# The fifth product of the second group of units 1 to 6 in the inner form, with exponentials, divisions, turns and the load of v in other slots

## The chip, the cores and the metric

The kernel runs on one core of one Trainium2 chip. The metric is the device time of one execution in microseconds; the time before is the median of three runs. The profile is one further execution under the hardware profiler. The engines are named as there: PE (matrix products), PEld (PE's loads of weights, which run beside its products), DVE (vector), ACT (scalar, with tables for functions), POOL (GpSimd) and SP (which issues DMAs).

## The reference

All data are float32. For each of 8 batches with 8 heads, 576 queries and head size 64, keys and values are pooled by 8 (72 keys), and attention is taken over them. The result, 4608 tokens by 512, goes through a layer with a periodic activation:

```python
k_p = k.reshape(B, H, Sp, pool, D).mean(axis=3)
v_p = v.reshape(B, H, Sp, pool, D).mean(axis=3)
scores = scale * np.matmul(q, k_p.transpose(0, 1, 3, 2))
scores = scores - np.max(scores, axis=-1, keepdims=True)
attn = np.exp(scores)
attn = attn / (np.sum(attn, axis=-1, keepdims=True) + 1e-09)
x = np.matmul(attn, v_p)                      # then (4608, 512)
h = x @ w_in                                  # (512, 2048)
s = np.sin(alpha * h)
g = h + s * s / (alpha + 1e-09)
out = g @ w_out                               # (2048, 512)
```

## The kernel before

**Two levels of seven products.** The products with `w_in` and `w_out` are cut into 2 x 2 blocks and done with seven block products and sums of blocks instead of eight block products (Winograd's form of Strassen's method). For `w_in` the outer blocks are two halves of the 512 inputs, two halves of the 2048 features, and two halves of 256 tokens of a unit. The nine units (u = 0 to 8) have 512 tokens each. In a unit the features go in four groups (J = 0 to 3), each of 2 x 128 features in each half. One of the seven products of one group is four matmuls of 128 x 128 weights by 256 tokens (`product`, line 866, `part` picks from the four). Its result stays in one of the banks b1, b6, b5 and b7 of the accumulation memory, which ACT copies one into the other (line 839: b6 from b1, b7 from b6, and p5 from b5) so that later products add to them. DVE then forms the blocks of h (line 838).

Some products are done in a second, inner level of the same form (`inner_product`, line 1046): seven matmuls of 128 x 128 by 128 tokens instead of four by 256 (line 1058). They come in four steps. Step a makes two products into a spare bank, and ACT copies them to the target bank (line 1062) and to a small tile m (line 1064). Step b makes two products, and ACT copies one quarter of the bank to another (line 1068). Step d makes one, and DVE adds m (line 1073). Step e makes the last two. Before the change the units 1 to 6 (`busy`) do the fifth product of the groups 2 and 3 and the first product of group 3 so (`I5, I1 = (2, 3), (3,)`). The sums of weight blocks that this needs are made once in unit 0 by POOL (`inner_w_in`, line 823 through `sums`), those of the tokens in each unit (`inner_x`).

**Slots.** `hidden(u, extra)` writes out by hand a unit's 28 slots, seven (k = 0 to 6) for each group, with one product in most. Each engine does its instructions in the order in which they are written. In group G's slots the group before, Q, is finished too: `sin` and `square` on ACT (lines 1028 and 1035, in place in the tile s), `finish` on DVE (line 1080), and `store_g`, which writes g to DRAM (line 1094). The product 1 stands in k = 0, 5 in k = 1, 6 in k = 2, 2 in k = 3, 7 in k = 4, 3 in k = 5 and 4 in k = 6. When the next group's fifth product is in the inner form, the second half of the fourth product is left to the next group's first slots.

**Attention between the slots.** `carry(u)` hangs the attention of the batch u + 1 into a unit's slots as extras: `two_scores` (slots 3 and 5) puts the scores into banks, and `shifts` on DVE subtracts the maximum into `ex` (lines 341 and 342). `exp` is four instructions on ACT in place (line 367), three of 576 columns and one of 864. `norm` sums and inverts on DVE (lines 373 and 374) and scales on POOL (line 375). `turn` transposes 32 x 32 blocks on DVE (lines 504 to 514), `move` sends the pieces to their partitions by DMA (line 524), and `all_values` multiplies with the pooled values. `load_v` asks for v (two DMAs at line 141, four at line 146), and POOL sums it by eight (`pool_rows`, line 132) in the place in its queue at which `load_v` is called.

**Tables.** Sine and exponential need different tables in ACT; a load is an instruction of its own (ACT_TABLE_LOAD), put ahead of the first instruction that needs another table than the one loaded. Squares and copies run with either.

**DMA queues.** All these DMAs are issued by SP in the order written. They use eight semaphores in turn, so that each issue also waits for the landing of the eighth before it.

Of the kernel before, what the change touches and what calls it, by code (L numbers as in the profile page):

```python
# [13 lines left out]
F32 = mybir.dt.float32  # L14
AX = mybir.AxisListType.X
AF = mybir.ActivationFunctionType
# [3 lines left out]
P = 128  # L20
# [20 lines left out]
class Kernel:  # L41
# [793 lines left out]
    def hidden(self, u, extra):  # L835
# [3 lines left out]
        copy = lambda o, x: nc.scalar.copy(out=o, in_=x)  # L839
        sin, square, early = self.sin, self.square, lambda G: G.J == (0 if G.u else 1)  # L840
        busy = 0 < u < self.B - 1
        I5, I1 = ((2, 3), (3,)) if busy else {7: ((2, 3), (2, 3)), 8: ((2, 3), (2, 3))}.get(u, ((), ()))
        split = lambda J: u == 0 and J == 2
        end = lambda J: u == 0 and J == 3

        def begin(J):
# [30 lines left out]
        for slot in range(7 * self.NJ):  # L877
# [9 lines left out]
            if k == 0:  # L887
# [3 lines left out]
                self.next = None  # L891
                if G.i5 and not N:
                    G.i5.a()
                if Q and not G.i5 and not end(J):
                    self.last_sines(Q, 2)
                extras()
                if G.i1:
                    G.i5.b()
                    self.last_sines(Q, 0)
                else:  # L900
                    product(G, 1, G.b1, True)
                    if G.i5:
                        product(Q, 4, Q.b7, part=(2, 3))
            elif k == 1:
                if not G.i1:
                    copy(G.b6[:], G.b1[:])
                if G.i5 and not G.i1:
                    self.last_sines(Q, 0)
                elif Q and not G.i1:
                    if end(J):  # L910
                        self.last_sines(Q, 2)
                    for i in (0,) if split(J) else (1, 0) if u == 0 else (0, 1):
                        squares(Q, i)
# [3 lines left out]
            elif k == 2:  # L917
                if Q and not G.i5 and not split(J):
                    self.finish(Q)
                if not G.i1:  # L920
                    extras()
                if G.i1:
                    product(G, 6, G.b6, part=(0, 1))
                    G.i5.d()
                    self.last_sines(Q, 1)
                    square(Q, 1, 0)
                    self.late = Q
                    extras()
                    self.finish_before()
                    product(G, 6, G.b6, part=(2, 3))  # L930
                elif G.i5:
                    product(G, 6, G.b6, part=(0, 1))
                    G.i5.b()
                    self.last_sines(Q, 1)
                    squares(Q, 0)
                    product(G, 6, G.b6, part=(2, 3))
                else:
                    product(G, 6, G.b6)
            elif k == 3:
                late = J == 0 and busy  # L940
                if Q and not late and not G.i5 and not split(J):
                    self.store_g(Q)
                G.p5 = self.tp.tile([P, JW, TH], F32, name="p5")
                if G.i1:
                    if not busy:
                        copy(G.b7[:], G.b6[:])
                    square(Q, 1, 1)
                    squares(Q, 0)
                    extras()
                    product(G, 2, G.b1)  # L950
                    G.i5.e()
                    copy(G.p5[:], G.b5[:])
                else:
                    copy(G.b7[:], G.b6[:])
                    if G.i5:
                        squares(Q, 1)
                        G.i5.d()
                        self.finish(Q)
                        self.store_g(Q)
                    else:  # L960
                        copy(G.p5[:], G.b5[:])
                    if split(J):
                        squares(Q, 1)
                        self.finish(Q, (0,))
                    extras()
                    product(G, 2, G.b1)
            elif k == 4:
                if G.i1 and busy:
                    copy(G.b7[:], G.b6[:])
                    self.behind_order = lambda: sin(G, 0, 0, G.b1)  # L970
                else:
                    sin(G, 0, 0, G.b1)
                if not G.i5:
                    square(G, 0, 0)
                extras()
                if G.i1:
                    self.finish(Q, (1,))
                    self.store_g(Q)
                product(G, 7, G.b7, part=(0, 1))
                if G.i5:  # L980
                    if not G.i1:
                        G.i5.e()
                        copy(G.p5[:], G.b5[:])
                    square(G, 0, 0)
                product(G, 7, G.b7, part=(2, 3))
            elif k == 5:
                add(G.g[:, 1, :, 1], G.b7[:], G.p5[:])
                extras()
                if split(J):
                    self.finish(Q, (1,))  # L990
                    self.store_g(Q)
                N = None
                if J + 1 in I1:
                    N = self.next = begin(J + 1)
                    N.i1.a()
                product(G, 3, G.b6, part=(0, 1))
                if N:
                    N.i1.b()
                product(G, 3, G.b6, part=(2, 3))
            else:  # L1000
                if J == 0 and busy and Q:
                    self.store_g(Q)
                add(G.g[:, 0, :, 1], G.b6[:], G.p5[:])
                sin(G, 1, 1, G.g[:, 1, :, 1])
                N = self.next
                last = lambda: add(G.g[:, 0, :, 0], G.b1[:], G.s[:, 0, :, 0])
                if not N:
                    last()
                    extras()
                    product(G, 4, G.b7, part=(0, 1))  # L1010
                    if J + 1 not in I5 or J + 1 in I1:
                        product(G, 4, G.b7, part=(2, 3))
                else:
                    product(G, 4, G.b7, part=(0,))
                    N.i1.d()
                    last()
                    N.i5.a()
                    product(G, 4, G.b7, part=(1, 2))
                    N.i1.e()
                    copy(N.b6[:], N.b1[:])  # L1020
                    extras()
                    product(G, 4, G.b7, part=(3,))
# [7 lines left out]
    def square(self, G, i, js):  # L1030

        for jj in range(JW):
            f = i * self.K2 // 2 + G.J * JW + jj
            x = G.s[:, i, jj, js, :]
            self.nc.scalar.activation(out=x, in_=x, func=AF.Square, scale=self.c[:, f:f + 1])  # L1035

    def last_sines(self, G, part):

# [163 lines left out]
    def carry(self, u):  # L1202
# [6 lines left out]
        if u == 0:  # L1209
# [37 lines left out]
            at(19, A.move, (3,), nc.scalar)  # L1247
            at(26, A.all_values)
            at(9, self.load_q, 2)
            at(23, lambda: self.inner_w_in(((5, 2, 4), (1, 3, 4)), (lambda w: [w[:, i * 2 * P:i * 2 * P + 2 * P] for i in range(8)])(self.q_tile(0))))  # L1250
            for e in range(2):
                at(12, self.load_k, 2, e)
                at(17, lambda e=e: self.pool_k[e]())
# [5 lines left out]
        if 0 < u < last:  # L1259
# [2 lines left out]
                at((3, 5)[i], A.two_scores, i)  # L1262
            at(6, A.two_shifts)
            for i in range(4):
                at((8, 9, 10, 10)[i], A.exp, i)
                at((9, 10, 11, 12)[i], A.norm, i)
                at((12, 13, 13, 13)[i], A.turn, i)
            at(14, A.move, range(4))
            at(6, self.load_v, b)
            at(12, lambda: self.pool_v())  # L1270
            for i in range(2):
                if b < last:
# [440 lines left out]
```

## Time and profile before

| | us |
|---|---|
| median of three runs | 900.68 |
| lowest, highest | 899.46, 901.40 |
| span of the profiled execution, first to last instruction | 896.2 |
| time of the profiled execution beside its span | not listed |
| PE busy | 890.8 |
| weight loads busy | 813.9 |
| DVE busy | 682.9 |
| ACT busy | 438.6 |
| POOL busy | 249.2 |

The units 1 to 6 take the stretch from about 82 to 409 us of the span, some 55 us each; from 513 us on PE works on the products with `w_out` alone. The granted PE clock is 1.000 over the span. In a timeline the columns are the start, the length, the engine, the line, the operation, what it writes and reads, the form, how many instructions follow each other (x), and in brackets the engine's idle time before them and what ended it. Each matmul of the program is two rows in the trace. SPq is SP's issue of a DMA, not the transfer.

### The profile page before, as it was taken

How to read it: one execution, taken by the hardware profiler on the slowest of the kernel's cores; microseconds unless marked ns; L12 is line 12 of the kernel's file. 1: busy time of each engine (PE TensorE's matmuls, PEld its weight loads, DVE VectorE, ACT ScalarE, POOL GpSimd, SP SyncE). 2: the span in 40 equal slices, each digit the busy share in tenths (PEclk: the TensorE clock that was granted, in tenths of full speed). 3: DMA queues.
4: the chain of work that ended last, by engine and by line, in shares of the span. 5: the costliest groups of instructions: out<-in, count | busy, mean ns of one | idle time of the engine just before them, and what ended most of it. 6: DMA issues, size and time to landing. Idle time of an engine off the chain costs nothing.

```text
span 896.2 us, 16276 instructions
## 1 busy us (share of the span) xinstructions
PE 890.8 (99%) x6274; PEld 813.9 (91%) x6274; DVE 682.9 (76%) x918; ACT 438.6 (49%) x1033; POOL 249.2 (28%) x265
## 2 busy tenths in 40 slices
PE   9999999999999999999999999999999999999998
PEld 6787888888888888888888999999999999999998
DVE  7786857768577675765677889898897896996885
ACT  6687776877768777687776711111111211111111
POOL 6798443825338252434523000000000000000000
PEclk9999999999999999999999999999999999999999
DMA  9857957759586585648126243716435355164002
GB/s 269 244 158 206 244 147 212 187 164 254 139 214 186 183 225 147 175 140 302 53 106 219 102 181 103 232 37 218 117 105 160 89 159 159 37 192 142 20 18 53
DMA packets 119533, 141.03 MB, mean 157 GB/s; under 512 B 45776, under 2 KB 86496, under 8 KB 119456
## 3 DMA queue, kind: packets, MB, share of 16 engines
q1 hardware_dynamic: 116288, 137.39, 52.6%
q10 hardware_dynamic: 3168, 2.61, 1.0%
q8 instruction: 50, 0.82, 0.4%
q14 instruction: 27, 0.22, 0.1%
HBM read 75.37 MB, written 47.19 MB: 137 GB/s over the span
## 4 chain that ended last, share of the span: by engine, by line
PE 99%; DVE 0%; POOL 0%; ACT 0%; issue 0%; DVEq 0%
PE PS L866 44%; PE PS L1383 43%; PE PS L1058 5%; PE PS L318 2%; PE PS L613 2%; PE PS L626 1%; PE PS L1126 0%; PE PS L571 0%; PE PS L290 0%; PE PS L425 0%; PE PS L279 0%; PE PS L479 0%; PE PS L569 0%; POOL tr L451 0%; PE PS L403 0%; PE PS L487 0%
## 5 line engine op out<-in xcount | busy, mean ns | idle before, releaser
L866 PE MATMUL PS<-home,a 128*128 128x256 f32 x1072 | 253.0, 381 | 0.1
L866 PEld LDWEIGHTS PS<-home,a 128*128 128x128 f32 x1072 | 198.4, 190 | 30.9 <-issue 4.6
L866 PE MATMUL PS<-home,as 128*128 128x256 f32 x736 | 177.2, 382 | 0.0
L866 PEld LDWEIGHTS PS<-home,as 128*128 128x128 f32 x736 | 134.5, 190 | 18.1 <-ACT PS L839 1.2
L1383 PE MATMUL PS<-s,wb 128*128 128x192 f32 x672 | 116.2, 326 | 0.0
L1035 ACT ACTIVATE s<-s,c 128x256 f32<-128x256 f32 (+1 forms) x236 | 115.5, 556 | 0.0
L1383 PEld LDWEIGHTS PS<-s,wb 128*128 128x128 f32 x672 | 110.4, 190 | 0.1
L132 POOL TENSOR_TENSOR kvin<-kvin 96x768 f32<-96x768 f32 (+3 forms) x42 | 73.4, 1747 | 69.9 <-DMA kvin<-in_v_dram 67.8
L838 DVE TENSOR_TENSOR h<-PS,p 128x512 f32<-128x512 f32 x72 | 49.2, 684 | 55.5 <-PE PS L866 35.2
L1554 ACT COPY PS<-PS 128x192 f32<-128x192 f32 x42 | 12.7, 303 | 146.2 <-PE PS L1383 130.0
L1028 ACT ACTIVATE s<-h,al 128x256 f32<-128x256 f32 x144 | 65.5, 509 | 32.6 <-DVE h L838 32.6
L1383 PE MATMUL PS<-r,wb 128*128 128x192 f32 x432 | 79.0, 326 | 0.0
L1383 PEld LDWEIGHTS PS<-r,wb 128*128 128x128 f32 x432 | 71.6, 190 | 0.0
L1383 PE MATMUL PS<-s,a 128*128 128x192 f32 x384 | 70.2, 326 | 0.0
L1028 ACT ACTIVATE s<-PS,al 128x256 f32<-128x256 f32 x144 | 60.0, 469 | 17.2 <-PE PS L866 16.5
L1383 PEld LDWEIGHTS PS<-s,a 128*128 128x128 f32 x384 | 63.7, 190 | 0.0
L1080 DVE TENSOR_TENSOR h<-PS,s 128x512 f32<-128x512 f32 x36 | 24.8, 689 | 48.6 <-ACT s L1035 48.6
L839 ACT COPY PS<-PS 128x512 f32<-128x512 f32 x72 | 41.5, 577 | 34.5 <-PE PS L866 26.7
L1080 DVE TENSOR_TENSOR h<-h,s 128x1024 f32<-128x1024 f32 x36 | 55.3, 1537 | 3.3 <-ACT s L1035 3.1
L1584 ACT COPY PS<-PS 128x192 f32<-128x192 f32 x42 | 12.7, 303 | 89.5 <-PE PS L1383 89.5
L1322 DVE TENSOR_TENSOR s<-r 128x768 f32<-128x768 f32 x54 | 51.4, 951 | 4.8 <-PE PS L1383 2.8
L1383 PE MATMUL PS<-s,we 128*128 128x192 f32 x288 | 52.7, 326 | 0.0
(244 smaller groups left out, 1401.4 us busy)
## 6 DMA issues: line engine op xcount, KB each, us to landing
g_bridge<-h SPq DMA_DIRECT2D x72, 512.0 KB
r<-g_bridge SPq DMA_DIRECT2D x15, 1536.0 KB
x<-g_bridge SPq DMA_DIRECT2D x8, 1536.0 KB
out_dram<-o SPq DMA_DIRECT2D x90, 96.0 KB
kvin<-in_k_dram SPq DMA_DIRECT2D x14, 576.0 KB
q<-in_q_dram SPq DMA_DIRECT2D x7, 1024.0 KB
kvin<-in_v_dram SPq DMA_DIRECT2D x14, 512.0 KB
aM<-tr SPq DMA_DIRECT2D x54, 92.0 KB
```

Of the source, the lines that this page charges most:

```text
L132: self.nc.gpsimd.tensor_tensor(out=t[..., 0:w] if w > D else out, in0=t[..., 0:w], in1=t[..., w:2 * w], op=OP.add)
L318: nc.tensor.matmul(ps[e][r0 + r:r0 + r + q.shape[-1], h, :], q[s], kb[s, hp, :], start=True, stop=True)
L613: nc.tensor.matmul(o[r:r + 64], w, x, start=start and i < 2, stop=False, skip_group_check=True)
L838: add = lambda o, x, y: nc.vector.tensor_tensor(out=o, in0=x, in1=y, op=OP.add)
L839: copy = lambda o, x: nc.scalar.copy(out=o, in_=x)
L866: nc.tensor.matmul(ps[:, jj, :], self.A[p][:, kk, f * P:(f + 1) * P], x[:, kk, :], start=(start and n == 0), stop=(kk == 1), skip_group_ch ...
L1028: self.nc.scalar.activation(out=G.s[:, i, jj, j, :], in_=src[:, jj], func=AF.Sin, scale=self.al[:, f:f + 1])
L1035: self.nc.scalar.activation(out=x, in_=x, func=AF.Square, scale=self.c[:, f:f + 1])
L1058: nc.tensor.matmul(o, W[m][:, G.J - J0], X[m], start=start and n == 0, stop=True, skip_group_check=True)
L1080: add = lambda o, x, y: self.nc.vector.tensor_tensor(out=o, in0=x, in1=y, op=OP.add)
L1322: tt = lambda o, x, y, op: nc.vector.tensor_tensor(out=o, in0=x, in1=y, op=op)
L1383: nc.tensor.matmul(out, W[:, J // 2, J % 2, :], A[:, J, :], start=(start and J == 0), stop=(J == self.NJ - 1), skip_group_check=True)
```

## The change

In the units 1 to 6 the group J = 1 joins those whose fifth product is in the inner form (`fast(G)` is true for it). Its slots are written out anew:

- k = 0: step a, then the sines of Q's first half (those on g), then product 1. The four matmuls of its fifth product are gone.
- k = 1: the copy into b6, a square of Q, step b, the second half of Q's fourth product (left over from J = 0), Q's sines from b7 and the wide squares.
- k = 2: half of product 6, step d, `finish(Q)`, the other half.
- k = 3: `store_g(Q)`, the copy into b7, half of product 2, step e, the extras, the copy to p5, the other half.
- k = 6: the sines of g's second half are left to J = 2, which does them in its k = 1.

The exponentials go in two runs: two in slot 6 (J = 0, k = 6) and two in slot 10, where all four were in the slots 8 to 10. Behind the first run stands a sine of one column (`sine_table`), which brings the sine's table back there. The divisions (`norm`) stand in the slots 7, 7, 10 and 12 (before 9, 10, 11 and 12), the turns in 9, 13, 13 and 13 (before 12, 13, 13 and 13). `load_v` moves from slot 6 to slot 4, ahead of a `store_g`. The sums of weights for the fifth product are made for three groups instead of two, in the same memory.

```diff
-        I5, I1 = ((2, 3), (3,)) if busy else {7: ((2, 3), (2, 3)), 8: ((2, 3), (2, 3))}.get(u, ((), ()))
+        I5, I1 = ((1, 2, 3), (3,)) if busy else {7: ((2, 3), (2, 3)), 8: ((2, 3), (2, 3))}.get(u, ((), ()))
         split = lambda J: u == 0 and J == 2
+        fast = lambda G: busy and G.J == 1
...
                 if G.i5 and not N:
                     G.i5.a()
+                if fast(G):
+                    sin(Q, 0, 1, Q.g[:, 0, :, 1])
...
                     product(G, 1, G.b1, True)
-                    if G.i5:
+                    if G.i5 and not fast(G):
                         product(Q, 4, Q.b7, part=(2, 3))
             elif k == 1:
                 if not G.i1:
                     copy(G.b6[:], G.b1[:])
-                if G.i5 and not G.i1:
+                if fast(G):
+                    square(Q, 0, 1)
+                    G.i5.b()
+                    product(Q, 4, Q.b7, part=(2, 3))
+                    self.last_sines(Q, 1)
+                    squares(Q, 1)
+                elif G.i5 and not G.i1:
+                    if fast(Q):
+                        sin(Q, 1, 1, Q.g[:, 1, :, 1])
                     self.last_sines(Q, 0)
...
+                if fast(G):
+                    product(G, 6, G.b6, part=(0, 1))
+                    G.i5.d()
+                    self.finish(Q)
                 if not G.i1:
                     extras()
-                if G.i1:
+                if fast(G):
+                    product(G, 6, G.b6, part=(2, 3))
+                elif G.i1:
...
-                if Q and not late and not G.i5 and not split(J):
+                if Q and not late and (not G.i5 or fast(G)) and not split(J):
                     self.store_g(Q)
...
-                    if G.i5:
+                    if fast(G):
+                        product(G, 2, G.b1, part=(0, 1))
+                        G.i5.e()
+                    elif G.i5:
...
                     extras()
-                    product(G, 2, G.b1)
+                    if fast(G):
+                        copy(G.p5[:], G.b5[:])
+                    product(G, 2, G.b1, part=(2, 3) if fast(G) else range(4))
...
-                if not G.i5:
+                if not G.i5 or fast(G):
                     square(G, 0, 0)
...
-                if G.i5:
+                if G.i5 and not fast(G):
...
-                sin(G, 1, 1, G.g[:, 1, :, 1])
+                if not fast(G):
+                    sin(G, 1, 1, G.g[:, 1, :, 1])
...
+    def sine_table(self):
+        self.nc.scalar.activation(out=self.sm.tile([P, 1], F32, name="order")[:], in_=self.al[:, 0:1], func=AF.Sin)
...
-            at(23, lambda: self.inner_w_in(((5, 2, 4), (1, 3, 4)), (lambda w: [w[:, i * 2 * P:i * 2 * P + 2 * P] for i in range(8)])(self.q_tile(0))))
+            at(23, lambda: self.inner_w_in(((5, 1, 4), (1, 3, 4)), (lambda w: [w[:, i * 3 * P:i * 3 * P + 3 * P] for i in range(4)] + [w[:, 12 * P + i * P:13 * P + i * P] for i in range(4)])(self.q_tile(0))))
...
             for i in range(4):
-                at((8, 9, 10, 10)[i], A.exp, i)
-                at((9, 10, 11, 12)[i], A.norm, i)
-                at((12, 13, 13, 13)[i], A.turn, i)
+                at((6,6,10,10)[i], A.exp, i)
+                at((7,7,10,12)[i], A.norm, i)
+            for i in range(4):
+                at((9,13,13,13)[i], A.turn, i)
+            at(6, self.sine_table)
             at(14, A.move, range(4))
-            at(6, self.load_v, b)
+            at(4, self.load_v, b)
```

## The prediction

> **What bounds the kernel now.** I read the page first: its busy shares and the chain that ended last. Then one unit in the window view, then the timelines of the engines for the second group (J = 1) of unit 3.
>
> ```profile
> span 896.2 us, 16276 instructions
> ...
> PE 890.8 (99%) x6274; PEld 813.9 (91%) x6274; DVE 682.9 (76%) x918; ACT 438.6 (49%) x1033; POOL 249.2 (28%) x265
> ...
> PE 99%; DVE 0%; POOL 0%; ACT 0%; issue 0%; DVEq 0%
> ```
> ```profile
> 150.59:205.66 55.07, 55.07 (x447) 47.22 (x446) 38.23 (x64) 41.13 (x96) 25.58 (x25) 1.00 0.71 192
> ```
>
> The chain is PE from end to end, and in the 55.07 us that separate a place in one unit from the same place in the next, PE is never idle; ACT is busy for 41.13. So a change is worth what it takes from PE's own work, minus what it makes PE wait. An average of 41 in 55 does not say whether ACT is free at one given place, so I follow it there.
>
> ```profile
> 207.42 3.62 PE L866 MATMUL PS<-home,a 128*128 128x256 f32 x16
> 210.87 3.62 PE L866 MATMUL PS<-home,as 128*128 128x256 f32 x16
> 214.32 3.66 PE L866 MATMUL PS<-home,a 128*128 128x256 f32 x16
> ...
> 220.41 0.39 PE L1058 MATMUL PS<-home,as 128*128 128x128 f32 x2
> 220.63 0.39 PE L1058 MATMUL PS<-last,q 128*128 128x128 f32 x2
> 220.86 2.75 PE L866 MATMUL PS<-home,a 128*128 128x256 f32 x12
> ...
> 223.45 1.09 PE L866 MATMUL PS<-home,as 128*128 128x256 f32 x4
> 224.38 0.38 PE L1058 MATMUL PS<-last,q 128*128 128x128 f32 x2
> ```
>
> Columns: start, length, what, count. Each matmul of the program is two rows of the trace. Sixteen of 256 columns start 3.45 us apart (207.42 to 210.87), 0.216 each, so a product (eight rows) takes 1.73. A product of the inner form (two rows of 128 columns) takes 0.22 (220.41 to 220.63 to 220.86: 0.45 for two). 207.42 is the fourth product of J = 0, 209.14 the first of J = 1, 210.87 its fifth and sixth, 214.32 its second and seventh, 220.41 step a of J = 2.
>
> **What PE saves.** The fifth product's 1.73 becomes seven inner products, 7 x 0.2225 = 1.56: 0.17 a unit. The row at 214.32 is 3.66 long where its like is 3.62: 0.04 is lost there to the copy into b7, which has more cover after. Together 0.21 a unit, 1.3 us over six units.
>
> **What ACT does for it.** These are its rows around the change, in the same unit and the next group:
>
> ```profile
> 205.02 0.91 ACT L1028 ACTIVATE s<-h,al 128x256 f32<-128x256 f32 x2 [0.88 <-DVE h L838]
> 208.34 0.91 ACT L1028 ACTIVATE s<-h,al 128x256 f32<-128x256 f32 x2 [2.42 <-DVE h L838]
> 209.16 0.89 ACT L1035 ACTIVATE s<-s,c 128x256 f32<-128x256 f32 x2
> 209.96 0.81 ACT L1028 ACTIVATE s<-PS,al 128x256 f32<-128x256 f32 x2
> 211.07 0.57 ACT L839 COPY PS<-PS 128x512 f32<-128x512 f32 x1 [0.30 <-PE PS L866]
> 211.55 1.33 ACT L1035 ACTIVATE s<-s,c 128x512 f32<-128x512 f32 x2
> 212.90 1.28 ACT L367 ACT_TABLE_LOAD   x1
> 214.20 1.26 ACT L367 ACTIVATE ex<-ex 128x576 f32<-128x576 f32 x2
> 215.36 0.58 ACT L839 COPY PS<-PS 128x512 f32<-128x512 f32 x1
> ...
> 221.48 0.37 ACT L1062 COPY PS<-PS 128x256 f32<-128x256 f32 x1
> 221.78 0.27 ACT L1064 COPY m<-PS 128x128 f32<-128x128 f32 x1
> 222.79 0.57 ACT L839 COPY PS<-PS 128x512 f32<-128x512 f32 x1 [0.74 <-PE PS L866]
> ...
> 225.08 0.25 ACT L1068 COPY PS<-PS 128x128 f32<-128x128 f32 x1 [0.90 <-PE PS L1058]
> ```
> ```profile
> L1121 ACT ACTIVATE one<-ident x1: 202/202/202, 3.0 to 3.0; 128x1 f32<-128x1 f32 x1
> ```
>
> Before, ACT rested from 205.93 to 208.34. After, this gap holds the first two exponentials and the sine of one column, and both need a table load, 1.28 each. Starts follow each other sooner than lengths say: a pair of sines on h holds the queue 0.82 (208.34 to 209.16), a pair of squares 0.80, a 512-wide copy 0.48, L1062's copy 0.30; the next instruction starts some 0.09 before the last ends. A load is the exception: it starts when the last has ended (211.55 + 1.33 = 212.88, load at 212.90) and holds what follows until it is done (214.20).
>
> The walk on ACT, from the sine at 205.02, whose start PE sets and which stays where it is: ends 205.93; load 205.94; two exponentials 207.24 to 208.50; load 208.51; the one-column sine 209.81, 0.20 long by the row of L1121, so the next at 209.92; step a's copy (L1062) 209.92 to 210.29; its second copy at 210.22, 0.27 long, less 0.09; the sines of the group before at 210.40; the copy from b1 to b6 at 211.21, ended 211.78; two squares at 211.69; step b's copy (L1068) 212.49, ended 212.74.
>
> The walk on PE, if nothing held it: half the fourth product from 207.42, step a 208.28, first product 208.73, step b 210.46, the other half of the fourth product 210.90, half the sixth 211.76, step d 212.63. Step b needs step a's copy (210.29), the sixth product the copy into b6 (211.78), step d step b's copy (212.74). PE asks before the matmul starts, with its weights:
>
> ```profile
> 215.99 1.59 PEld L866 LDWEIGHTS PS<-home,a 128*128 128x128 f32 x8 [0.18 <-ACT PS L839]
> ...
> 220.20 0.41 PEld L1058 LDWEIGHTS PS<-home,as 128*128 128x128 f32 x2
> ```
>
> Weights go out 0.21 ahead of the matmul (220.20, 220.41), and 0.05 after the copy that held them (215.36 + 0.58 = 215.94, 215.99). For step d: 212.74 + 0.05 + 0.21 = 213.00, and up to 0.05 more where the wait stands in an instruction of its own. Against 212.63 that is 0.37 to 0.42; I take 0.40. The smaller waits at step b (some 0.1) and at the sixth product lie inside it, for ACT runs without a gap from 205.02 to step b's copy and its end is what counts. Such holds exist already: in J = 2 the copy at 222.79 ends 223.36, the four rows at 223.45 last 1.09 and the next start 0.93 later instead of 0.87, 0.06 lost.
>
> Bounds of this price: the one-column sine could hold the queue for 0.05 only, and its neighbour 0.16 instead of 0.18: delay 0.29. Without the overlaps (0.09 twice) and with sines a tenth slower, 0.65. I take 0.40 since every other term is a row of this kind and place.
>
> **Behind step d** everything keeps its cover. ACT: the sines from b7 at 212.65, the wide squares 213.38 to 214.71, the copy into b7 at 214.62 to 215.20 (seventh product not before 216.3), load, the other two exponentials 216.50 to 217.99, the copy to p5 to 218.48, load, the sines of b1 at 219.78, squares, and step a of J = 2 at 221.3, where it was 221.48. The second pair of loads thus falls into time that had no work on PE's path; on PE's path they would cost 2.6 a unit. The sines moved from J = 1 to J = 2 (0.82) fit between the copy into b6 there and step b's copy at 225.08, which waits for PE.
>
> **DVE, POOL and SP.** DVE gains step d's add and does divisions and turns elsewhere:
>
> ```profile
> 209.91 1.06 DVE L342 TENSOR_TENSOR ex<-PS,mx 128x864 f32<-128x864 f32 x1
> 213.53 1.22 DVE L1080 TENSOR_TENSOR h<-h,s 128x1024 f32<-128x1024 f32 x1
> 217.06 0.76 DVE L373 TENSOR_REDUCE sm<-ex 128x8 f32<-128x584 f32 x1 [0.29 <-ACT ex L367]
> 218.03 0.69 DVE L838 TENSOR_TENSOR h<-PS,p 128x512 f32<-128x512 f32 x1
> 218.63 0.70 DVE L504 STREAM_TRANSPOSE tr<-ex 128x512 f32<-128x512 f32 x1
> ...
> 229.26 1.93 DVE L1080 TENSOR_TENSOR h<-h,s 128x1024 f32<-128x1024 f32 x1
> ```
> ```profile
> 211.30 4.58 POOL L132 TENSOR_TENSOR kvin<-kvin 128x1024 f32<-128x1024 f32 x2 [10.57 <-DMA kvin<-in_v_dram]
> 215.95 0.73 POOL L132 TENSOR_TENSOR vm<-kvin 128x256 f32<-128x256 f32 x1
> 216.64 3.37 POOL L375 TENSOR_TENSOR ex<-ex,sm 128x576 f32<-128x576 f32 x3
> ```
> ```profile
> 196.73 5.42 SPq L1094 DMA_DIRECT2D g_bridge<-h  x4
> 202.24 1.44 SPq L141 DMA_DIRECT2D kvin<-in_v_dram  x2
> ```
>
> DVE: shifts done 210.97, two divisions' halves (0.9 each) to 212.8, the add of step d at 213.4, the finishing adds at 214.75 (after the squares) to 216.6, the first turn (0.8) to 217.4, the third division to 218.3, then the add on b7 and p5 at 218.5 to 219.2. The second half of PE's fourth product follows at 219.36 + 0.40, so 0.4 is spare. It needs the first turn not to wait: POOL must have pooled v (5.3 from its start) and scaled the first tile (1.12) by 216.6, so v must be in SBUF by 210.1, and by 210.7 to cost nothing. It was there at 211.30. SP now asks for v ahead of two of the four stores in the row at 196.73, from about 198 instead of 202.24, and two transfers fewer lie ahead of it; I take 206 to 208. The two stores passed go out some 2 us later, and the h buffer they free is next written at 218.5. The query's load behind them waits for the scores anyway. The finishing add can last 1.93 when POOL works beside it (229.26): 0.7, inside the 0.28 before the p5 copy and the 0.4.
>
> [...]
>
> Unit 0's sums for three groups instead of two lengthen four POOL instructions by half, below 2 us once:
>
> ```profile
> 84.74 0.46 POOL L823 TENSOR_TENSOR last<-home 128x128 f32<-128x128 f32 x1 [3.66 <-DVE home L833]
> ```
>
> POOL idles 3.66 behind them, so they cost nothing.
>
> **Sum.** A unit: 0.40 - 0.21 = +0.19; six units +1.1 us, a span of 897.3 after 896.2. The median of the three runs, 900.68 (899.46 to 901.40), is 4.5 above the profiled span, which stands for the launch's rest; the profiled execution has no other time listed. Forecast 901.8, slower by 0.13%, which a measurement of this kernel can hardly tell from no change (0.2%, 1.8 us). With the bounds of the delay the likeliest case's own range is 901.2 to 903.3.
>
> **Rivals.**
> (1) ACT is in time and only the saving shows: -1.3, 899.4. It needs step b's copy ended by 212.37, 0.37 sooner. For it: the exponentials stand where ACT rested 2.4 us. Against: two loads and two exponentials take 3.9. 0.14, a third of it (waits of before that vanish besides) below 898.9.
> (2) The first turn holds DVE: v lands no sooner than 211.30, POOL's first scaling ends 217.8, turn 218.6, third division 219.5, add 220.2 instead of 219.2; PE's fourth product loses 0.6 a unit more, 3.6: 905.4. It decides from a landing after 210.7. For it: DMA is 71% busy in the unit and v takes 9 us from its issue to 211.30. Against: it is asked 4 us sooner. 0.17, with the slow finishing add.
> (3) A switch of the table holds ACT as long again as its load: 1.28 more each, 2.56 in ACT's walk, step d 2.96 late, 2.75 net a unit, 16.5 us: 917. Against: the rows at 211.55, 212.90 and 214.20 leave 0.02 on either side of the load. 0.02. [...]
> (4) The inner form runs no faster here and ACT holds nothing: 900.7. 0.05.
>
> The forecast has 0.62; some 0.22 of that, delays above 0.51, is over 902.5. Faster by over 0.2%: 0.05 of (1) and 0.02 of (4), 0.07. Slower by over 0.2%: 0.22 + 0.17 + 0.02 = 0.41. Within: 0.52. The range reaches from the saving alone, 899.4, to near (2), 904.8.
>
> **What would show it.** In the profile after: a weight load of step d in J = 1 idle before it for about 0.3 with ACT L1068's copy as its releaser, six times; four table loads a unit instead of two; ACT without a gap between the sines at the end of J = 0 and step b's copy; POOL's pooling of v starting before 210 on this unit's scale; DVE's add on b7 and p5 ready before PE's fourth product. Wrong if PE shows no idle there, or if the largest wait is DVE behind POOL.

## The result: slower, and the time after

| | us |
|---|---|
| after, median of six runs | 905.43 (902.60 to 909.03) |
| before, on the same chip, six runs | 899.11 (898.29 to 901.40) |
| ratio | 1.0066, 95% interval 1.0044 to 1.0088 |
| profiled execution after | 907.65, span 905.9 |

The kernel is slower by 0.66%, where 0.13% was forecast, and 905.43 lies above the range. Its runs also spread over 6.4 us, twice as far as those before. In the kernel after, the lines of the code have moved: L866 is now L867 (product), L1058 is L1084 (inner product), L1062, L1064 and L1068 are L1088, L1090 and L1094 (the copies of steps a and b), L1028 and L1035 are L1051 and L1058 (sine and square), L1080 is L1106, L1061 is the one-column sine.

From the page of the kernel after: the span, the busy times and the chain that ended last.

```profile
span 905.9 us, 16407 instructions
...
PE 895.1 (99%) x6310; PEld 816.3 (90%) x6310; DVE 679.3 (75%) x924; ACT 459.1 (51%) x1069; POOL 245.1 (27%) x265
...
PE 98%; issue 1%; DMA 0%; DVE 0%; POOL 0%; ACTq 0%; ACT 0%; DVEq 0%; POOLq 0%
```

The chain is PE still, with one new part: 1% "issue", in which PE waited for nothing that the profile shows. It is not spread evenly. In the window view, cut where PE begins the value products (L613) of each unit, the columns are the stretch, its length, the busy time of each engine, the granted clock, the DMA share and GB/s:

```profile
132.52:187.71 55.19, 55.19 (x455) 47.09 (x458) 37.86 (x65) 44.47 (x102) 24.77 (x25) 1.00 0.67 192
187.71:246.66 58.95, 56.89 (x456) 48.40 (x458) 37.54 (x65) 44.73 (x102) 24.76 (x25) 0.97 0.64 180
246.66:302.05 55.39, 55.39 (x455) 47.02 (x458) 37.92 (x65) 44.47 (x102) 24.77 (x25) 1.00 0.66 191
302.05:359.67 57.62, 55.12 (x455) 47.47 (x458) 37.66 (x65) 44.62 (x102) 24.73 (x25) 1.00 0.65 184
359.67:414.87 55.20, 55.20 (x455) 47.10 (x458) 35.67 (x63) 44.47 (x102) 17.19 (x19) 1.00 0.52 149
```

Before, the same five stretches take 55.07, 55.06, 55.25, 55.07 and 55.06. Three of them are longer by 0.12 to 0.14, two by 3.89 and 2.55. These five are the units 2 to 6. Together they are 6.84 longer; all that lies ahead of them is 2.60 longer and the rest 0.26, which makes the 9.7 between the spans. Of the 2.60, unit 1 has 0.13 (53.66 after 53.53), and 2.46 stand ahead of it. There PE's program is the same in both, and PE waits 0.8 for the first query's transfer; in the other kernels below the first value products begin at 76.6 to 78.5 on the span's scale (76.3 before, 78.8 here), so this part changes from execution to execution.

**The quiet stretches are what was forecast.** ACT in the timeline of unit 1, the rows that answer to the walk of the prediction (its 205.02 is 97.34 here, 107.68 less):

```profile
97.34 0.91 ACT L1051 ACTIVATE s<-h,al 128x256 f32<-128x256 f32 x2 [0.88 <-DVE h L838]
98.27 1.28 ACT L367 ACT_TABLE_LOAD   x1
99.56 1.26 ACT L367 ACTIVATE ex<-ex 128x576 f32<-128x576 f32 x2
100.84 1.28 ACT L1061 ACT_TABLE_LOAD   x1
102.13 0.20 ACT L1061 ACTIVATE order<-al 128x1 f32<-128x1 f32 x1
102.24 0.37 ACT L1088 COPY PS<-PS 128x256 f32<-128x256 f32 x1
102.54 0.26 ACT L1090 COPY m<-PS 128x128 f32<-128x128 f32 x1
102.70 0.90 ACT L1051 ACTIVATE s<-h,al 128x256 f32<-128x256 f32 x2
103.51 0.58 ACT L839 COPY PS<-PS 128x512 f32<-128x512 f32 x1
104.02 0.90 ACT L1058 ACTIVATE s<-s,c 128x256 f32<-128x256 f32 x2
104.83 0.26 ACT L1094 COPY PS<-PS 128x128 f32<-128x128 f32 x1
```

Every start lies within 0.03 of the walk (step b's copy 104.83 against 212.49 - 107.68 = 104.81), there is no gap, and each load starts 0.02 after what is ahead of it has ended. PE in the same place:

```profile
103.05 0.39 PE L1084 MATMUL PS<-home,as 128*128 128x128 f32 x2
103.27 1.03 PE L867 MATMUL PS<-home,a 128*128 128x256 f32 x4
104.14 1.13 PE L867 MATMUL PS<-home,as 128*128 128x256 f32 x4
105.23 0.46 PE L1084 MATMUL PS<-last,q 128*128 128x128 f32 x2
105.52 1.03 PE L867 MATMUL PS<-home,as 128*128 128x256 f32 x4
```

And the weights of step d:

```profile
105.20 0.30 PEld L1084 LDWEIGHTS PS<-last,q 128*128 128x128 f32 x2 [0.33 <-issue]
```

The sixth product starts at 104.14 and step d 1.09 later, where four such rows take 0.87; step d's own two take 0.29 instead of 0.22. With 0.04 at step b, that is 0.34 a unit, at the sixth product and at steps b and d. 0.34 less the 0.21 saved is 0.13, which the quiet stretches show. The idle time of 0.33 ahead of step d's weights is the sign that the prediction named, with one difference: the view gives "issue" as its end, and not ACT's copy. The copy ends at 105.09, and the weights start 0.11 later. This idle time stands in the units 1, 2, 4 and 6, and in all six of the kernel below with v and the first turn where they were.

### The profile page after: what moved, and what is told of

Read it like the earlier page. It is cut to its first block, busy times and chain, and to the rows that moved or that the text cites. A ratio compares the mean times of both kernels' runs of the same rounds, so it can differ in the third digit from the quotient of the medians.

```text
span 905.9 us, 16407 instructions
## 1 busy us (share of the span) xinstructions
PE 895.1 (99%) x6310; PEld 816.3 (90%) x6310; DVE 679.3 (75%) x924; ACT 459.1 (51%) x1069; POOL 245.1 (27%) x265
## 4 chain that ended last, share of the span: by engine, by line
PE 98%; issue 1%; DMA 0%; DVE 0%; POOL 0%; ACTq 0%; ACT 0%; DVEq 0%; POOLq 0%
PE PS L867 43%; PE PS L1411 42%; PE PS L1084 6%; PE PS L318 2%; PE PS L613 2%; PE PS L626 1%; DMA q<-in_q_dram 0%; PE PS L425 0%; PE PS L571 0%; PE PS L290 0%; PE PS L279 0%; PE PS L479 0%; PE PS L569 0%; POOL tr L451 0%; PE PS L403 0%
## 5 line engine op out<-in xcount | busy, mean ns | idle before, releaser
L867 PE MATMUL PS<-home,a 128*128 128x256 f32 x1072 | 256.2, 381 | 0.1
L867 PEld LDWEIGHTS PS<-home,a 128*128 128x128 f32 x1072 | 198.0, 191 | 29.6 <-issue 4.6
L867 PE MATMUL PS<-home,as 128*128 128x256 f32 x688 | 169.5, 385 | 0.0
L867 PEld LDWEIGHTS PS<-home,as 128*128 128x128 f32 x688 | 125.2, 191 | 19.8 <-issue 3.1
L1058 ACT ACTIVATE s<-s,c 128x256 f32<-128x256 f32 (+1 forms) x236 | 115.5, 556 | 0.0
L132 POOL TENSOR_TENSOR kvin<-kvin 96x768 f32<-96x768 f32 (+3 forms) x42 | 71.2, 1696 | 44.0 <-DMA kvin<-in_v_dram 42.2
L1051 ACT ACTIVATE s<-h,al 128x256 f32<-128x256 f32 x144 | 65.0, 509 | 18.4 <-DVE h L838 18.3
L1051 ACT ACTIVATE s<-PS,al 128x256 f32<-128x256 f32 x144 | 60.1, 470 | 17.3 <-PE PS L867 16.4
L839 ACT COPY PS<-PS 128x512 f32<-128x512 f32 x72 | 41.6, 578 | 35.5 <-PE PS L867 27.7
L1106 DVE TENSOR_TENSOR h<-PS,s 128x512 f32<-128x512 f32 x36 | 24.9, 691 | 42.8 <-ACT s L1058 42.8
L1106 DVE TENSOR_TENSOR h<-h,s 128x1024 f32<-128x1024 f32 x36 | 47.8, 1329 | 3.3 <-ACT s L1058 3.1
```

The lines of the kernel that those rows point to most:

```text
L132: self.nc.gpsimd.tensor_tensor(out=t[..., 0:w] if w > D else out, in0=t[..., 0:w], in1=t[..., w:2 * w], op=OP.add)
L867: nc.tensor.matmul(ps[:, jj, :], self.A[p][:, kk, f * P:(f + 1) * P], x[:, kk, :], start=(start and n == 0), stop=(kk == 1), skip_group_ch ...
L1051: self.nc.scalar.activation(out=G.s[:, i, jj, j, :], in_=src[:, jj], func=AF.Sin, scale=self.al[:, f:f + 1])
L1106: add = lambda o, x, y: self.nc.vector.tensor_tensor(out=o, in0=x, in1=y, op=OP.add)
```

## Where the long stretches come from

In the timeline of PE in the units 3 and 5, J = 0, at the second pair of scores:

```profile
206.85 1.52 PE L318 MATMUL PS<-kblk,q 64*64 64x72 f32 x79
210.44 0.22 PE L318 MATMUL PS<-kblk,q 64*64 64x72 f32 x1 [2.06 <-issue]
210.59 3.21 PE L867 MATMUL PS<-home,as 128*128 128x256 f32 x8
213.60 1.53 PE L867 MATMUL PS<-home,a 128*128 128x256 f32 x4
...
321.18 1.09 PE L318 MATMUL PS<-kblk,q 64*64 64x72 f32 x53
324.77 0.71 PE L318 MATMUL PS<-kblk,q 64*64 64x72 f32 x27 [2.50 <-issue]
```

PE stops in the middle of a run of alike matmuls: for 2.06 before its 80th and last row in one unit, for 2.50 before its 54th in the other. No semaphore stands there. Of DMA, in two windows of the DMA view of the same kernel (queue, kind, packets, MB, share):

```profile
DMA packets 1184, 2.24 MB, mean 255 GB/s; under 512 B 88, under 2 KB 88, under 8 KB 1184
q1 hardware_dynamic: 1184, 2.24, 95.8%
...
DMA packets 257, 0.50 MB, mean 335 GB/s; under 512 B 19, under 2 KB 19, under 8 KB 256
q1 hardware_dynamic: 256, 0.49, 96.7%
q8 instruction: 1, 0.02, 5.4%
```

The first two rows are of 199 to 207.8 us, the others of 207.8 to 209.3. The page lists q8, kind "instruction", with 50 packets and 0.82 MB, 16,384 bytes each. From one packet to the next there are 256 of PE's instructions in the trace (from 499 to 891 us 4,864 rows of weight loads, matmuls and semaphores in 19 packets). So these packets are PE's program: block by block, 256 instructions at a time. Counted that way, one can say for each block at which instruction it is asked for, when its packet starts, and how long PE takes for the 256 instructions up to the place where it needs it:

```
kernel        unit  asked for  packet starts   late   256 take   PE idle
before          3     199.69      200.74       1.05     5.56       -
before          5     309.78      310.97       1.19     5.54       -
after           3     202.24      207.90       5.66     5.55      2.06
after           5     313.76      322.09       8.33     7.97      2.50
v_soon_alone    3     199.95      203.60       3.65     5.56       -
v_soon_alone    5     310.04      315.71       5.67     5.54      2.18
moved_blocks    4     257.58      263.12       5.54     5.55      1.50
moved_blocks    6     367.08      374.07       6.99     7.35      1.76
v_late          3     202.14      203.37       1.22     5.55       -
v_late          5     312.55      316.70       4.16     7.97       -
v_turn_late     3     200.54      201.75       1.21     5.55       -
v_turn_late     5     308.64      312.88       4.24     8.15       -
```

(The times are worked out, to some 0.2, from the trace's packets and from the count of PE's rows, in which the 154th of each 256 is taken as the place where the next block is asked for: in none of the eleven traces does a packet start more than 0.2 ahead of it. The last eight rows are of experiments below.) Elsewhere behind the opening, 256 instructions take 11 to 26 us in the kernel after, and a packet that starts late costs nothing: two there start 5.80 and 7.50 after their requests (at 238.62 and 388.74), and no stop of PE follows. Two blocks more are short there, 6.87 in unit 1 and 6.66 in unit 6; their packets start 1.02 and 3.16 after the request, and PE does not stop. The scores are 80 rows of 0.02 in each run, with a weight load for each, so a block that holds them lasts 5.5 to 8 us only. In the kernel before, v's two transfers of 512 KB are asked for at 202.24, behind that block's request at 199.69. In the kernel after they go out at 200.3, ahead of it at 202.24; the block then waits almost until they are through (its packet starts at 207.90, and POOL begins on v at 209.02). In all five cases PE moves on 2.54 to 2.68 us after its packet's start, and all five stops stand at one place, the 193rd row of a 256. Behind the opening, no other block of the eleven traces has less than 3.9 from its packet's start to that row. In unit 5 the order is less clear: two stores go out at 313.54, the block is asked for at 313.76 and v at 314.53, and yet the packet starts at 322.09 only, 1.2 before POOL begins on v. So either transfers that go out somewhat later delay a block too, or the request is later than it is taken here. The theory, then: **v asked for sooner stands in the way of PE's own program.**

Each block is by this count asked for about as the one before it begins: the 154th row lies 39 ahead of the 193rd, where the stops stand. No run here shows more than one block asked for ahead.

One stop cost more than its own length. The windows around the two stops, granted clock in the third column from the end:

```profile
210.40:214.00 3.60, 3.56 (x10) 2.74 (x10) 0.16 (x1) 2.30 (x4) 2.96 (x3) 0.61 0.75 235
...
324.80:328.00 3.20, 3.20 (x39) 2.84 (x39) 0.55 (x1) 2.23 (x4) 2.84 (x3) 1.00 0.59 183
```

Behind the stop of unit 3 the clock is 0.61 on average over 3.6 us and the matmuls take longer (eight rows 3.21 instead of 1.89), another 1.7 in all; behind the longer stop of unit 5 it is 1.00. Of the six runs the longest, 909.03, has the lowest mean clock, 0.994, and the shortest, 902.60, has 1.000, which points to the clock behind the stops as a large part of the spread.

## Experiments

The rival to the blocks theory is that the new slots (exponentials, divisions, turns) make the two long stretches, or that PE waits there for data that arrive later. The first four kernels ran together.

**v where it was, all else as after.**

```diff
-            at(4, self.load_v, b)
+            at(6, self.load_v, b)
```

> The changed kernel with v asked for at slot 6, where it was; PE's program is the same row for row. Blocks theory: PE's program comes from memory in blocks of 256 instructions (16,384 bytes, queue 8 of the trace); a block that is asked for while v's transfers fill the DMA engines starts 5.7 and 8.3 us late, and in unit 3 and unit 5 PE runs through the block before it in 5.6 and 8 us because it holds the scores. With v late again the block is asked for ahead of v's transfers: no idle above 1 us before the scores (L318), all units near 55.2, and 900 to 901.5 us, 4 to 5 below the changed kernel. Slots theory (the exponentials, divisions and turns in their new places make the two long units): they stay, 905. If v now holds the first turn (rival 2 of the prediction), every unit gains 0.6 and the time is 904, with DVE behind POOL as the releaser.

Measured 906.18 against 898.96, ratio 1.0077 (1.0064 to 1.0090). The stops at the scores are gone, as the table above shows; the time is not. The waits of PE in this kernel (place, releaser: us in all, times, longest), and DVE and POOL in unit 3:

```profile
PE PS L867 <- DVE h L838: 4.9, 5, 1.5
```
```profile
220.95 0.71 DVE L504 STREAM_TRANSPOSE tr<-ex 128x512 f32<-128x512 f32 x1 [1.73 <-POOL ex L375]
```
```profile
214.28 3.71 POOL L132 TENSOR_TENSOR kvin<-kvin 128x1024 f32<-128x1024 f32 x2 [10.91 <-DMA kvin<-in_v_dram]
```

POOL gets v at 214.28, the first turn waits 1.73 for POOL, and the add on b7 and p5 behind it holds PE's fourth product (its first half, which the prediction and the expectations call the second). That is rival 2 of the prediction, at 1.1 to 1.8 a stretch (56.58, 56.64, 56.96 and 56.27 against 55.2) instead of 0.6. So v at slot 4 has a use as well as a price: with the first turn at slot 9, v is needed early.

**v sooner, and nothing else**, in the kernel before:

```diff
-            at(6, self.load_v, b)
+            at(4, self.load_v, b)
```

> The kernel before with v asked for at slot 4 and nothing else. Blocks theory: v's transfers are in flight when the blocks of units 3 and 5 are asked for (due at 199.7 and 309.8 in the trace of before, needed 5.6 us later), so PE idles about 2 us at the scores in one or both units: 901 to 905 us. Slots theory: nothing changes but v's arrival, 899 to 900.

Measured 903.11, ratio 1.0038 (1.0025 to 1.0050). One move of a load, with no arithmetic changed, costs some 4 us (2.2 to 4.5 by the interval). In the profile one stretch is 59.20 long, the other four are 55.06 to 55.25:

```profile
314.70 1.47 PE L318 MATMUL PS<-kblk,q 64*64 64x72 f32 x77
318.34 0.34 PE L318 MATMUL PS<-kblk,q 64*64 64x72 f32 x3 [2.18 <-issue]
318.61 3.68 PE L866 MATMUL PS<-home,as 128*128 128x256 f32 x8
```

The stop is 2.18, at the same scores, in unit 5, and the clock behind it is 0.55 on average over 3.6 us (the eight rows at 318.61 take 3.68). The slots theory, which had 899 to 900 here, falls.

**The blocks moved.** 48 matmuls more in the opening, so that every block begins 96 instructions earlier in the program; v at slot 4 as after. `fill` takes a width and a count of pieces, so that one wide and 55 narrow multiplications stand where eight wide ones were:

```diff
-        fill(5)
+        fill(1)
+        fill(30, 64, 1)
...
-        fill(3)
+        fill(25, 64, 1)
```

> The changed kernel with 96 more PE instructions in the opening, where PE has nothing to do: 48 narrow multiplications more in the place of wide ones. Nothing after the opening changes but where the blocks of 256 instructions begin, 96 instructions earlier. Blocks theory: the trace of the changed kernel, with the blocks cut 96 earlier, has no block that is both asked for behind v's transfers and needed within the time they take; no idle above 1 us at the scores of units 3 and 5, 900.5 to 902. If PE waits for v's or the query's data there, or for the new slots: the two long units stay, 905.

Measured 903.31, ratio 1.0047 (1.0033 to 1.0061). The stops in the units 3 and 5 are gone, as expected; that there would be none elsewhere was wrong. They stand in the units 4 and 6, which were quiet:

```profile
263.60 0.70 PE L867 MATMUL PS<-home,as 128*128 128x256 f32 x2
265.80 1.46 PE L867 MATMUL PS<-home,as 128*128 128x256 f32 x6 [1.50 <-issue]
...
373.85 1.11 PE L318 MATMUL PS<-kblk,q 64*64 64x72 f32 x56
376.72 0.66 PE L318 MATMUL PS<-kblk,q 64*64 64x72 f32 x24 [1.76 <-issue]
```

One of them is in a run of products now, not at the scores. What stops PE is therefore not an instruction's data but the place of the block's end, and the units that are hit change with the program's length ahead of them. A unit has 922 of PE's instructions (910 before), 3.6 blocks, so the blocks' ends wander from unit to unit; two of the six were hit either way. The clock stayed at 1.00 behind both stops, and the time is 2 below that of the kernel after.

**The inner form without the early exponentials**: v, exponentials, divisions and turns in the slots before, no one-column sine.

```diff
-                at((6,6,10,10)[i], A.exp, i)
-                at((7,7,10,12)[i], A.norm, i)
+                at((8, 9, 10, 10)[i], A.exp, i)
+                at((9, 10, 11, 12)[i], A.norm, i)
...
-                at((9,13,13,13)[i], A.turn, i)
+                at((12, 13, 13, 13)[i], A.turn, i)
-            at(6, self.sine_table)
...
-            at(4, self.load_v, b)
+            at(6, self.load_v, b)
```

> The fifth product of the second group in the inner form, with the exponentials, divisions, turns and v where they were before and no sine to load a table. ACT has no exponentials ahead of step b's copy then, so step d finds it: the 0.3 us that PE loses there in a quiet unit of the changed kernel go, and PE saves 0.2 a unit: 897.5 to 898.5. If the two exponentials now hold the copy into b7 or into p5 for PE, 0.3 to 1 a unit is lost in J = 1 at the seventh product instead: 899 to 904. Blocks theory: no idle above 1 us at the scores. Slots theory: the same.

Measured 906.71, ratio 1.0086 (1.0072 to 1.0099): the second case. No stop at the scores, and the gaps at steps b and d are gone, but PE waits for the copy into b7 in every unit, as ACT and PE of unit 3 show:

```profile
217.54 1.28 ACT L367 ACT_TABLE_LOAD   x1
218.83 1.26 ACT L367 ACTIVATE ex<-ex 128x576 f32<-128x576 f32 x2
220.00 0.58 ACT L839 COPY PS<-PS 128x512 f32<-128x512 f32 x1
```
```profile
218.35 1.03 PE L867 MATMUL PS<-home,a 128*128 128x256 f32 x4
220.63 1.56 PE L867 MATMUL PS<-home,a 128*128 128x256 f32 x6 [1.25 <-ACT PS L839]
```

The load and two exponentials ahead of the copy make a stretch of 56.37, 1.31 over the kernel before. So the early exponentials are needed for the inner form, the early turn needs the early v, and the early v costs the stops.

**v and the first turn where they were, the rest as after.** This takes away what made v urgent.

```diff
-                at((9,13,13,13)[i], A.turn, i)
+                at((12, 13, 13, 13)[i], A.turn, i)
...
-            at(4, self.load_v, b)
+            at(6, self.load_v, b)
```

> The changed kernel with v asked for at slot 6 and the first turn at slot 12, both as before; the exponentials, the divisions and the inner form stay as changed. Blocks theory: without v's transfers ahead of them the instruction blocks come in time, no idle above 1 us at the scores; and with the turn behind the add on b7 and p5, DVE holds nothing, so the 1.4 us a unit of the run with v late alone goes. All units 55.2, of which PE loses 0.34 at four places in J = 1 to ACT: 899.5 to 900.5 us, 0.5 to 1.5 above the kernel before. If the long units come from the slots of the exponentials and divisions: two units of 57 to 59, 905.

Measured 899.93 against 898.94, ratio 1.0012 (1.0003 to 1.0021), 0.5% below the kernel after. PE's waits are those of the opening, but for one:

```profile
PE PS L1152 <- DVE full L1625: 1.1, 1, 1.1
PE PS L213 <- DMA h<-in_v_dram: 1.0, 1, 1.0
PE PS L1084 <- ACT PS L1088: 0.2, 1, 0.2
```

The stretches are 55.20, 55.70, 55.43, 55.20 and 55.20. The 55.43 holds 0.18 that the kernel before has too (55.25), and in the stretch of 55.70, unit 3, 0.33 goes at step b to ACT's copy, the wait in the last line. With the stops away, the inner form with early exponentials costs 1.0 (0.3 to 1.9 by the interval), near the 1.1 that the prediction's sum had for the whole change.

**One exponential ahead instead of two**, on top of that:

```diff
-                at((6,6,10,10)[i], A.exp, i)
-                at((7,7,10,12)[i], A.norm, i)
+                at((6, 10, 10, 10)[i], A.exp, i)
+                at((7, 10, 11, 12)[i], A.norm, i)
```

> As the last, and the second exponential waits with the third and fourth at slot 10, its division at slots 10 and 11. ACT comes to step b's copy 0.58 sooner, more than the 0.34 that PE loses to it, so all four gaps in J = 1 go and only the saving of 0.21 a unit is left: units of 54.86 to 54.9, 897.5 to 898.5 us, 0.6 to 1.3 below the kernel before. If ACT is not what holds step d, units stay at 55.2 and the time at 900. If the three exponentials in a row hold the copy into p5 or step a of J = 2, as much as 0.5 a unit is lost there: 900 to 902.

Measured 899.38, ratio 1.0005 (0.9996 to 1.0014): no difference from the kernel before, where 0.6 to 1.3 less was expected. The gaps at the sixth product and at the steps b and d are gone in five of the six units (in unit 3, 0.13 stays at step d), which shows that ACT made them, and the last unit's stretch is the expected one:

```profile
351.94:406.86 54.92, 54.92 (x452) 47.27 (x451) 36.61 (x63) 44.56 (x102) 18.11 (x19) 1.00 0.51 146
```

The other stretches are 55.47, 55.38, 55.11 and 55.15. In the second and the fourth, 0.17 and 0.20 go at the first half of the fourth product, where DVE does a division's sum ahead of the add on b7 and p5. In the first, 0.45 goes at the value products, whose moves come later with the turns. The 0.19 of the third stands where the kernel before has it too.

Three more orders were tried to win these tenths. **The add first and all turns behind the two adds** (`norm` 7, 10, 12, 12; `turn` 13, 13, 13, 13):

> As the run with one exponential ahead, but the third division's sum stands behind the add on b7 and p5, and all four turns behind the two adds that follow, so that DVE does the adds first. In the run with one exponential PE lost 0.17 to 0.20 at the second half of its fourth product in three units to that add, and 0.45 once at the first value products, whose moves were late. If the add was late because of the division's sum, those 0.2 go and units are 54.9: 898.0 to 898.8 us. If the later turns hold the moves instead, the 0.45 at the value products comes in more units: 899.5 to 901.

901.06, ratio 1.0024 (1.0015 to 1.0033): the second case. In unit 2 SP issues the moves 41.6 after the first value product, 0.7 later than with one exponential ahead, and the first four stretches are 55.56, 55.53, 56.01 and 55.21.

**The second exponential ahead of the copy into b7** (`exp` 6, 8, 10, 10; `norm` 7, 9, 10, 12):

> As the run with one exponential ahead, but the second exponential stands at slot 8, ahead of the copy into b7, and its sum at slot 9; the first turn at slot 12 and v at slot 6 as there. ACT reaches step b's copy as early as there, so the four gaps of J = 1 stay away; the second sum no longer stands between the third exponential and the add on b7 and p5, and the moves are as early as with two exponentials ahead. The copy into b7 ends 1.3 us later, some 1.5 us ahead of what the seventh product needs. Units of 54.9, 897.8 to 898.7 us, below the kernel before by 0.3 to 1.1. If the copy into b7 is late for the seventh product: up to 0.3 a unit, 899.5 to 900.5.

903.76, ratio 1.0053 (1.0040 to 1.0067). The expectation had put the seventh product where the third stands, 1.7 too late. PE of unit 2:

```profile
163.15 1.99 PE L867 MATMUL PS<-home,a 128*128 128x256 f32 x8 [0.68 <-ACT PS L839]
```

The copy into b7 ends 163.10 and holds the seventh product in every unit; stretches of 55.8 and more.

**The add first, the turn where it was** (`norm` 7, 10, 12, 12; `turn` 12, 13, 13, 13):

> As the run with one exponential ahead, with one exchange on DVE: the third division's sum (0.95) behind the add on b7 and p5 instead of ahead of it; the first turn stays at slot 12. The 0.17 to 0.20 that PE lost at the second half of its fourth product in three units go; the moves stay where they were, so the value products keep their waits of up to 0.45. Five units of 54.9 to 55.2, 898.5 to 899.2 us, within 0.05% of the kernel before. If the add also waits for the copy into p5, the 0.2 stay and nothing changes: 899.4.

904.08 against 899.59, ratio 1.0048 (1.0035 to 1.0062), where 898.5 to 899.2 was expected. With both sums behind the first add, DVE comes to the second add, on b6 and p5, 37.5 after the unit's first value product, 0.75 later than in the run with one exponential ahead. Only then can the copy into b6 of the next group be made, and PE waits for that copy in each unit:

```profile
171.15 1.13 PE L867 MATMUL PS<-home,as 128*128 128x256 f32 x4 [0.76 <-ACT PS L839]
```

In the orders tried here each tenth won at one of these places is lost at the next; none beats the kernel before.

## Why the prediction was wrong

- **What PE saves, 0.21 a unit: right.** The last stretch with one exponential ahead is 54.92, 0.14 below the kernel before, and 0.07 of the rest stands in one place, the first half of the fourth product.
- **What ACT does for it, 0.40 at step d: mechanism right, 0.34 measured**, each row of the walk within 0.03. The one-exponential run shows the cause: with 0.58 less ahead, the gaps go in five of six units.
- **"Behind step d everything keeps its cover": right.** PE's waits in the kernel after hold nothing there. Each table load takes 1.28 and holds ACT no longer than that: the load at 98.27 starts 0.02 after the sine has ended, and the exponential at 99.56 0.01 after the load.
- **DVE, POOL and SP: the times right, one user of the queue missing. This is the step that failed.** v is at POOL at 100.00 in unit 1, 207.68 on the scale of the walk, where 206 to 208 stood; the first turn does not wait, and the add on b7 and p5 comes at 110.86 against 218.5 - 107.68 = 110.82. The pair of 1.22 and 1.93 for the finishing add does not show POOL's part by itself, for POOL is at work beside both (211.30, for 4.58); in the kernel after it takes 1.22 with POOL idle (107.71) and 1.54 with POOL at work (121.72). But the sentence that v is asked for some 4 us sooner was weighed only by what stands behind it on SP, two stores and the query's load. The page of before had the instruction packets, and PE's program was not counted among what those transfers delay: its delay was put at nothing, without a reason. Its price was 1.5 to 4.1 in each unit that was hit: two units in both kernels profiled with the inner form and v at slot 4, and one with v sooner alone.
- **The sum: 1.1 was right for the rest** (1.0 with v and the first turn where they were). What is missing in it is the 5 us between that run and the kernel after. The 4.5 between span and median is not the launch's rest: the kernel after takes 907.65 with a span of 905.9, 1.75 more. The median of three that the forecast of 901.8 starts from was high; six runs give 899.11.
- **Rivals.** (1) and (4) did not come. (2) did not either; that its time, 905.4, is near is chance: the largest wait is not DVE behind POOL. It is what comes with v late, at 1.1 to 1.8 a unit where the prediction had 0.6: v is at POOL 0.35 later in the unit, and POOL's last step of pooling takes 1.74 there (218.07 to 219.81) instead of 0.73. (3) did not.

## What to carry to other kernels

PE's program is a DMA load too (here 50 packets of 16,384 bytes): when transfers are asked for sooner, look in the trace for the "instruction" packets and ask which block they push back, above all where many short instructions (here matmuls of 0.02 us) use up a block in 5.5 to 8 us. An idle of the bound engine inside a run of alike instructions, with "issue" as its releaser (here 1.50 to 2.50), pointed there; adding instructions far ahead and seeing the stop wander (here by 96, from the units 3 and 5 to 4 and 6) told it from a wait for data. A load that is moved ahead to feed a step that was itself moved ahead should be tried with both left where they were.

## What was not expected of the hardware

- PE's program arrives in packets of 16,384 bytes, and data that go out at about the same time delay them: at the same two blocks the packet starts 1.05 and 1.19 us after its request in the kernel before, and 5.66 and 8.33 after it in the kernel after, where v's megabyte goes out 2.0 ahead of the request and 0.8 behind it. From the packet's start to PE's next instruction 2.54 to 2.68 us pass.
- A stop of PE of 2.06 and one of 2.18 us are followed by 3.6 us at a granted clock of 0.61 and 0.55 on average; behind stops of 1.50, 1.76 and 2.50 it is 1.00. The clock records of the trace show where the longest differs: in the kernel after the clock changes only at whole steps of 3.413 us from its first record (at 9.82, 211.20, 214.62 and 904.11), and it is 0.50 for one such step behind the stop of 2.06. That stop lies whole in one step (207.79 to 211.20); that of 2.50 is split, 1.57 and 0.93. With v sooner alone the clock is 1.00 from 315.90 to 318.30 and 0.55 on average in the 3.6 behind, which agrees with one step of 0.50 and with a stop of 2.18 that lies whole in the step ahead of it. So in these traces a step with 2.06 idle is followed by one at half clock, and steps with 1.57 and 0.93 are not; how much idle time in between is enough is not shown.
- What stays open: why the opening takes 76.3 to 78.8 us in these profiles, with the same program but for the filler of the moved blocks, and how stops and clock share out in the runs without a profile. Which of the transfers ahead of a block (two stores of 512 KB, v's two, v's rest) weighs most was not tried apart; with v behind, at the same block of unit 5, the packet is 4.16 and 4.24 late.
